# Reciprocal sums multiplied into the exponentials on GpSimd, and post mixing in matmuls of 256 columns

## The chip, the cores and the metric

The kernel runs on one core of a Trainium2 chip. The metric is the device time of one execution in microseconds; three runs were taken and the median is quoted. Beside them stands one execution under the hardware profiler, from which all rows of the trace come. The engines are called TensorE (PE in the profile, its weight loads PEld), VectorE (DVE), ScalarE (ACT), GpSimd (POOL) and SyncE (SP).

## The reference

Talking-heads attention (the heads are mixed before and after the softmax) for 4 batches, 12 heads, 448 positions and 64 channels per head, and then a mixer block: a token MLP over the 448 positions and a channel MLP over the 768 channels, both with a residual.

```python
scores = scale * np.matmul(q, k.transpose(0, 1, 3, 2))
scores = np.einsum('bhij,hg->bgij', scores, w_pre)
scores = scores - np.max(scores, axis=-1, keepdims=True)
attn = np.exp(scores)
attn = attn / (np.sum(attn, axis=-1, keepdims=True) + 1e-09)
attn = np.einsum('bhij,hg->bgij', attn, w_post)
x = np.matmul(attn, v)               # then heads side by side: (4, 448, 768)
h = np.maximum(x.transpose(0, 2, 1) @ w_tok1, 0.0) @ w_tok2
u = x + h.transpose(0, 2, 1)
out = u + np.maximum(u @ w_ch1, 0.0) @ w_ch2
```

## The kernel before

The attention is cut into 16 tiles (4 batches, each with 120, 120, 120 and 88 query rows), and a tile into groups of 10 query rows (the last of a batch ends with a group of 8). A group holds 10 rows of all 12 heads in 120 partitions. `steps` are one or two groups; there are 92 of them, 88 with two groups and 4 with one. The order of all instructions is written by hand (`manual_schedule`): the loop near the end of the attention issues, for step `i`:

- `regroup`: DMAs on SyncE that gather the score rows of later groups into one of 8 buffers `rt`.
- `pre` of step `i + 2`: matmuls with `kpre`, which mix the heads before the softmax, into PSUM (`PP`). `x` counts the two halves of a group's 10 rows, 5 rows and 12 heads (60 partitions of 64) each, `s` the groups of the step.
- `rec` of step `i + 1`: on VectorE 1e-9 is added to the sums (one instruction for each `x`) and the reciprocals are taken; then GpSimd multiplies `kpost` (the weights of the mixing after the softmax, 128 x 64) with the reciprocals, once for each `x`, into the tiles `wr`.
- `mx` of step `i + 2` (row maxima, VectorE), then for some steps `qk` (a later tile's scores, TensorE, copied out of PSUM by ScalarE), then `ex` of step `i + 2` (exponentials with their sums, ScalarE, one for each `x`, into one of the 6 tiles `et`).
- `post` of step `i`: matmuls with `wr` as weights, of 128 columns, 16 for each `x` where the step has two groups. Each stands as two instructions in the trace, each with a weight load of its own.
- `turn` of step `i`: VectorE transposes the result out of PSUM, in 32 x 32 blocks, into `AT`.
- `av` for some steps: the product of a finished tile's weights with `v`, for a pair of heads, from the tile before. Its result leaves PSUM by a copy on ScalarE and, by `settle` in the next step, an add on VectorE.

PSUM tiles of `qk`, `post` and `av` take turns in two buffers (`ps_w`), those of `pre` in two others. From the last tile of the attention on, `cv_tick` converts the weights of the mixer block, a unit at a time, on ScalarE, VectorE and GpSimd (`cv_clamp` and the low half in `cv_step`). The token MLP (`tok1`, `tok2`) and the channel MLP (`ch1`, `ch2`) follow; the change does not touch them.

Of the kernel before, what the change touches and what calls it, by code (L numbers as in the profile page):

```python
# [8 lines left out]
F32 = mybir.dt.float32  # L9
F32R = mybir.dt.float32r  # L10
BF16 = mybir.dt.bfloat16
I32 = mybir.dt.int32
U32 = mybir.dt.uint32
ACTF = mybir.ActivationFunctionType
ALU = mybir.AluOpType
# [4 lines left out]
B, H, S, D = 4, 12, 448, 64  # L20
DM = H * D
DT, DC = 256, 1536
JT = 4
# [1 line left out]
GR = 10  # L25
HP = H // 2
NR = 8
NE = 6
KD = DM // 128
NC = DC // 128  # L30
WARM = 11
# [6 lines left out]
def attn_mixer_kernel(  # L38
# [12 lines left out]
    nc = tc.nc  # L51
# [24 lines left out]
    mid = en("mid", bufs=2)  # L76
# [3 lines left out]
    kcat = [mid.tile([128, 34], F32, bufs=1, name=f"kcat{i}") for i in range(2)]  # L80
    kpre = mid.tile([128, 64], F32, bufs=1, name="kpre")
    kpost = mid.tile([128, 64], F32, bufs=1, name="kpost")
    et = [mid.tile([128, 512], F32, bufs=1, name=f"e{i}") for i in range(NE)]
    rt = [mid.tile([128, S], F32, bufs=1, name=f"r{i}") for i in range(NR)]
    AT, V = {}, {}

    K = {}
    Q = {}
    S_t, R, E, SM, WR, PP, PO = {}, {}, {}, {}, {}, {}, {}
    ne = [0]  # L90

    groups = []
# [86 lines left out]
    def ex(st):  # L179
        m = 64 * len(st)  # L180
        s, p = SM[st[0]], PP.pop(st[0])
        E[st[0]] = []
        for x in range(2):
            e = et[ne[0] % NE]
            ne[0] += 1
            nc.scalar.activation(  # L186
                out=e[:m, :S], in_=p[:m, x, :S], func=ACTF.Exp, bias=s[:m, x:x + 1], scale=1.0,
                accum_out=s[:m, 2 + x:3 + x],
            )
            E[st[0]].append(e)  # L190

    def rec(st):
        m = 64 * len(st)
        s = SM.pop(st[0])
        for x in range(2):
            nc.vector.tensor_scalar_add(out=s[:m, 4 + x:5 + x], in0=s[:m, 2 + x:3 + x], scalar1=1e-9)  # L196
        nc.vector.reciprocal(out=s[:m, 6:8], in_=s[:m, 4:6])  # L197
        WR[st[0]] = []
        for x in range(2):
            r = mid.tile([128, 64], F32, tag="wr", bufs=4, name="wr")  # L200
            nc.gpsimd.tensor_scalar(  # L201
                out=r[:m], in0=kpost[:m], scalar1=s[:m, 6 + x:7 + x], scalar2=None, op0=ALU.mult,
            )
            WR[st[0]].append(r)

    def post(st):
        p = pair("w", "post")
        for x, (e, w) in enumerate(zip(E.pop(st[0]), WR.pop(st[0]))):
            ek = e.rearrange("p (m a r) -> p m a r", m=JT, a=4)
            for hf in range(2):  # L210
                o = 256 * x + 128 * hf
                for a in range(4):
                    for s in range(len(st)):
                        k = slice(64 * s, 64 * s + 64)
                        nc.tensor.matmul(  # L215
                            out=p[32 * a:32 * a + 32, s, o:o + 128], lhsT=w[k, 32 * hf:32 * hf + 32],
                            rhs=ek[k, :, a, :], start=True, stop=True,
                        )
        PO[st[0]] = p

    def turn(st):
# [16 lines left out]
    def av(T, hp):  # L238
        settle()
        b, t = divmod(T, 4)  # L240
        i0, n = IT[t]
        w = 24 if t < 3 else 18
        at_ = AT[T].rearrange("p c (x f) -> p (c x) f", x=2)
        p = pair("w", "av")
        for j in range(JT):
            for r in range(2 if j < 3 else 1):
                k = slice(64 * r, 64 * r + 64)
                for s in range(2):
                    h = 2 * hp + s
                    f = 128 * (h // 6) + 32 * j + 5 * (h % 6)  # L250
                    nc.tensor.matmul(  # L251
                        out=p[64 * s:64 * s + 64, r, :5 * w], lhsT=V[b][k, h, j, :], rhs=at_[k, :w, f:f + 5],
                        start=j == 0, stop=j == 3 - r,
                    )
        x = late.tile([128, 120], F32, tag="x", bufs=6, name="x")
        m = n // GR * GR
        cols = [(x[:, :m].rearrange("p (k c) -> p c k", k=GR), lambda y: y[:, :m].rearrange("p (c k) -> p c k", k=GR))]
        if m < n:
            cols.append((x[:, m:n], lambda y: y[:, m + 1:n + 1]))
        for o, v_ in cols:  # L260
            nc.scalar.copy(out=o, in_=v_(p[:, 0]))

        def add():
            for o, v_ in cols:
                nc.vector.tensor_tensor(out=o, in0=v_(p[:, 1]), in1=o, op=ALU.add)
            nc.sync.dma_start(out=x_dr[b][:, hp, i0:i0 + n], in_=x[:, :n])

        pend.append(add)
# [11 lines left out]
    for r in rt:  # L280
        nc.gpsimd.memset(r[:4], 0.0)
    load_q(1, one)
    wz = et[0].bitcast(BF16)
    for e in et:
        nc.vector.memset(e if e is et[0] else e[:, S:], 0.0)
    for i in range(WARM):
        p = pair("w", "pw")
        nc.tensor.matmul(out=p[:120, 0], lhsT=wz[:120, :120], rhs=wz[:120, 120:632], start=True, stop=True)
# [2 lines left out]
    for x in range(2):  # L291
        ps_ = slice(64 * x, 64 * x + 64)
        nc.vector.tensor_tensor(
            out=kpre[ps_, :60].rearrange("p (i g) -> p i g", i=5),
            in0=kcat[0][ps_, :12].unsqueeze(1).to_broadcast([64, 5, H]),
            in1=mask[0][ps_, 5 * x:5 * x + 5].unsqueeze(2).to_broadcast([64, 5, H]), op=ALU.mult,
# [3 lines left out]
    for s in range(2):  # L300
        ps_ = slice(64 * s, 64 * s + 64)
        for hf in range(2):
            nc.gpsimd.tensor_tensor(
                out=kpost[ps_, 32 * hf:32 * hf + 30].rearrange("p (g i) -> p g i", g=6),
# [138 lines left out]
    for T in range(2, NT):  # L443
        f = sf[T - 2]
# [239 lines left out]
```

## Time and profile before

| | us |
|---|---|
| median of 3 runs | 835.3 |
| lowest, highest | 832.13, 836.86 |
| profiled execution | 840.8 |
| its span, first to last instruction | 839.0 |

Times in the rows are microseconds from the start of the span unless marked ns. In a timeline a row is a run of equal instructions of one engine, with its start, its length and, in brackets, the idle time of the engine before it and what ended it; "issue" means that the profile shows nothing that was waited for. Matmuls are pipelined and their ends are modelled. In a table of stretches each engine has its busy time and the number of its instructions; PEclk is the granted clock of TensorE as a share of the full one. A name such as post<-e,wr gives what an instruction writes and what it reads. The attention steps take the stretch from about 25 to 388 us.

### The profile page before, as it was taken

To read this page: it belongs to the slowest core of one execution; us is meant where nothing else is said; L and a number is where in the kernel's file an instruction comes from. 1 tells how busy PE (TensorE), PEld (TensorE's weight loads), DVE (VectorE), ACT (ScalarE), POOL (GpSimd) and SP (SyncE) were. 2 spreads that over 40 slices of the span, in tenths; PEclk is the share of its full clock that TensorE was granted. 3 is DMA by queue.
4 is the path that set the end of the run, shared out by engine and by line. 5 is a ranking of instruction groups with operands and counts; after the bars stand their busy time and mean duration, and the time that the engine had idled before them with its cause. 6 is when DMAs were issued, how large, how long until landed. Compare 5 with 4: busy or idle time off the path is not lost.

```text
span 839.0 us, 28093 instructions
## 1 busy us (share of the span) xinstructions
PE 799.1 (95%) x12091; PEld 619.8 (74%) x12091; DVE 478.1 (57%) x970; ACT 339.2 (40%) x817; POOL 194.6 (23%) x292
## 2 busy tenths in 40 slices
PE   7898898999999899987999999999999999999998
PEld 3455564666556565655788899999999999999997
DVE  3876576777777577886789999973000400030002
ACT  3666565666656566644455434431000200010000
POOL 3222121222222122223626777730000000000000
PEclk9999999999999999997799999999999999999999
DMA  5674456654765455365456676644000300010001
GB/s 170 204 227 138 117 166 194 212 134 146 224 194 145 113 181 179 128 145 185 134 170 225 184 204 176 172 151 169 1 1 1 132 0 1 1 67 1 1 0 66
DMA packets 63388, 106.05 MB, mean 126 GB/s; under 512 B 21747, under 2 KB 49952, under 8 KB 62752
## 3 DMA queue, kind: packets, MB, share of 16 engines
q1 hardware_dynamic: 62848, 103.35, 40.0%
q8 instruction: 95, 1.56, 0.8%
q10 hardware_dynamic: 320, 0.87, 0.4%
q14 instruction: 29, 0.24, 0.1%
q0 software_dynamic: 96, 0.03, 0.0%
HBM read 49.18 MB, written 16.52 MB: 78 GB/s over the span
## 4 chain that ended last, share of the span: by engine, by line
PE 51%; DVE 1%; ACT 0%; issue 0%
PE pc L522 7%; PE pc L521 7%; PE pc L523 7%; PE po L522 7%; PE po L521 7%; PE po L523 7%; PE pt L521 3%; PE pt L522 2%; PE pt L523 2%; PE pt L536 1%; PE tr L506 1%; PE av L251 1%; DVE ur L622 0%; PE pt L535 0%; DVE h L518 0%; DVE xn L513 0%
## 5 line engine op out<-in xcount | busy, mean ns | idle before, releaser
L518 DVE SCALAR_TENSOR_TENSOR rl<-pc,rh 128x448 fp32r<-128x448 f32 x48 | 29.8, 622 | 221.6 <-ACT rh L517 221.6
L228 DVE STREAM_TRANSPOSE at<-post 128x1024 f32<-128x1024 f32 (+1 forms) x92 | 112.8, 1226 | 73.3 <-PE post L215 73.1
L215 PEld LDWEIGHTS post<-e,wr 64*32 64x32 f32 x5760 | 84.6, 106 | 84.4 <-POOL wr L201 57.0
L201 POOL TENSOR_SCALAR wr<-kpost,sm 128x64 f32<-128x64 f32 (+1 forms) x184 | 79.0, 445 | 290.2 <-DVE sm L197 148.1
L186 ACT ACTIVATE e<-pre,sm 128x448 f32<-128x448 f32 (+1 forms) x184 | 115.2, 634 | 24.8 <-DVE sm L176 24.6
L215 PE MATMUL post<-e,wr 64*32 64x128 f32 x5760 | 114.3, 276 | 10.7 <-issue 7.1
L517 ACT ACTIVATE rh<-pc 128x448 fp32r<-128x448 f32 x48 | 26.1, 543 | 238.4 <-PE pc L523 238.4
L251 PE MATMUL av<-at,v 64*64 64x120 f32 (+1 forms) x2688 | 104.7, 274 | 14.1 <-issue 9.1
L148 ACT COPY s<-qk 120x896 f32<-120x896 f32 (+1 forms) x84 | 75.5, 906 | 95.0 <-PE qk L141 88.1
L169 PE MATMUL pre<-r,kpre 60*64 60x448 f32 (+1 forms) x720 | 108.1, 563 | 3.6 <-DMA r<-s 2.0
L141 PE MATMUL qk<-k,q 64*64 64x448 f32 (+2 forms) x768 | 104.1, 552 | 5.1 <-issue 1.8
L176 DVE TENSOR_REDUCE sm<-pre 128x2 f32<-128x896 f32 (+1 forms) x92 | 100.1, 1088 | 10.5 <-PE pre L169 6.4
L251 PEld LDWEIGHTS av<-at,v 64*64 64x64 f32 x2688 | 81.3, 137 | 32.4 <-issue 13.8
L522 PE MATMUL pc<-u,w 128*128 128x448 f32 x288 | 105.2, 365 | 0.0
L521 PE MATMUL pc<-u,w 128*128 128x448 f32 x288 | 105.2, 365 | 0.0
L523 PE MATMUL pc<-u,w 128*128 128x448 f32 x288 | 105.2, 365 | 0.0
L523 PE MATMUL po<-rh,w 128*128 128x448 f32 x288 | 105.2, 365 | 0.0
L521 PE MATMUL po<-rh,w 128*128 128x448 f32 x288 | 105.2, 365 | 0.0
L522 PE MATMUL po<-rl,w 128*128 128x448 f32 x288 | 105.2, 365 | 0.0
L390 POOL TENSOR_SCALAR cv_g<-cv_g 128x384 f32<-128x384 f32 (+2 forms) x56 | 87.1, 1556 | 21.7 <-ACT cv_g L384 21.7
L141 PEld LDWEIGHTS qk<-k,q 64*64 64x64 f32 (+2 forms) x768 | 37.2, 130 | 44.7 <-DVE sm L196 26.7
L521 PEld LDWEIGHTS pc<-u,w 128*128 128x128 f32 x288 | 54.1, 188 | 4.4
(70 smaller groups left out, 981.2 us busy)
## 6 DMA issues: line engine op xcount, KB each, us to landing
r<-s SPq DMA_DIRECT2D x176, 210.0 KB
cv_r<-in_w_ch_dram SPq DMA_DIRECT2D x48, 384.0 KB
v<-in_v_dram SPq DMA_DIRECT2D x16, 384.0 KB
xr<-x_dr SPq DMA_DIRECT2D x8, 672.0 KB
u_dr<-u SPq DMA_DIRECT2D x24, 224.0 KB
ur<-u_dr SPq DMA_DIRECT2D x4, 1344.0 KB
out_dram<-ur SPq DMA_DIRECT2D x24, 224.0 KB
k<-in_k_dram SPq DMA_DIRECT2D x21, 224.0 KB
```

Of the source, the lines that this page charges most:

```text
L141: nc.tensor.matmul(out=p[c:c + m, s, :S], lhsT=Q[T][r, h, c:c + m], rhs=K[b][r, h, :], start=True, stop=True)
L169: nc.tensor.matmul(out=p[64 * s:64 * s + 64, x, :S], lhsT=kpre[k], rhs=rt[a % NR][k], start=True, stop=True)
L176: nc.vector.tensor_reduce(out=s[:m, 0:2], in_=PP[st[0]][:m, :, :S], axis=AX.X, op=ALU.max, negate=True)
L186: nc.scalar.activation(out=e[:m, :S], in_=p[:m, x, :S], func=ACTF.Exp, bias=s[:m, x:x + 1], scale=1.0, accum_out=s[:m, 2 + x:3 + x],)
L201: nc.gpsimd.tensor_scalar(out=r[:m], in0=kpost[:m], scalar1=s[:m, 6 + x:7 + x], scalar2=None, op0=ALU.mult,)
L215: nc.tensor.matmul(out=p[32 * a:32 * a + 32, s, o:o + 128], lhsT=w[k, 32 * hf:32 * hf + 32], rhs=ek[k, :, a, :], start=True, stop=True,)
L228: nc.vector.transpose(out=AT[T][:, c:c + w].rearrange("p c f -> p (c f)"), in_=p[:, :w].rearrange("p c f -> p (c f)"))
L251: nc.tensor.matmul(out=p[64 * s:64 * s + 64, r, :5 * w], lhsT=V[b][k, h, j, :], rhs=at_[k, :w, f:f + 5], start=j == 0, stop=j == 3 - r,)
L390: nc.gpsimd.tensor_scalar(out=g[:P], in0=g[:P], scalar1=MAG_MIN, scalar2=MAG_MAX, op0=ALU.max, op1=ALU.min,)
L521: nc.tensor.matmul(out=p, lhsT=a[0], rhs=x[0], start=first, stop=False)
L522: nc.tensor.matmul(out=p, lhsT=a[0], rhs=x[1], start=False, stop=False)
L523: nc.tensor.matmul(out=p, lhsT=a[1], rhs=x[0], start=False, stop=last)
```

## The change

The reciprocals are no longer multiplied into the weights `kpost` but into the exponentials themselves, in place, by one GpSimd instruction for a step (2 x 448 columns, both `x` at once). With that the weights of `post` are `kpost` for both `x`, and one matmul takes the 128 columns of both: 256 columns, 16 matmuls for a step of two groups in place of 32. The two exponentials of a step now lie in one tile, so there are 3 tiles `et` of double width in place of 6. The two sums get their 1e-9 in one VectorE instruction. The order of the result's columns in `AT` changes with it, and `av` reads its operand with three strides (12 x 2 x 5) in place of two (24 x 5).

```diff
-NE = 6
+NE = 3
...
-    et = [mid.tile([128, 512], F32, bufs=1, name=f"e{i}") for i in range(NE)]
+    et = [mid.tile([128, 2, 512], F32, bufs=1, name=f"e{i}") for i in range(NE)]
...
     def ex(st):
         m = 64 * len(st)
         s, p = SM[st[0]], PP.pop(st[0])
-        E[st[0]] = []
+        e = et[ne[0] % NE]
+        ne[0] += 1
         for x in range(2):
-            e = et[ne[0] % NE]
-            ne[0] += 1
             nc.scalar.activation(
-                out=e[:m, :S], in_=p[:m, x, :S], func=ACTF.Exp, bias=s[:m, x:x + 1], scale=1.0,
+                out=e[:m, x, :S], in_=p[:m, x, :S], func=ACTF.Exp, bias=s[:m, x:x + 1], scale=1.0,
                 accum_out=s[:m, 2 + x:3 + x],
             )
-            E[st[0]].append(e)
+        E[st[0]] = e
 
     def rec(st):
         m = 64 * len(st)
-        s = SM.pop(st[0])
-        for x in range(2):
-            nc.vector.tensor_scalar_add(out=s[:m, 4 + x:5 + x], in0=s[:m, 2 + x:3 + x], scalar1=1e-9)
+        s, e = SM.pop(st[0]), E[st[0]]
+        nc.vector.tensor_scalar_add(out=s[:m, 4:6], in0=s[:m, 2:4], scalar1=1e-9)
         nc.vector.reciprocal(out=s[:m, 6:8], in_=s[:m, 4:6])
-        WR[st[0]] = []
-        for x in range(2):
-            r = mid.tile([128, 64], F32, tag="wr", bufs=4, name="wr")
-            nc.gpsimd.tensor_scalar(
-                out=r[:m], in0=kpost[:m], scalar1=s[:m, 6 + x:7 + x], scalar2=None, op0=ALU.mult,
-            )
-            WR[st[0]].append(r)
+        nc.gpsimd.tensor_tensor(
+            out=e[:m, :, :S], in0=e[:m, :, :S], in1=s[:m, 6:8].unsqueeze(2).to_broadcast([m, 2, S]), op=ALU.mult,
+        )
 
     def post(st):
         p = pair("w", "post")
-        for x, (e, w) in enumerate(zip(E.pop(st[0]), WR.pop(st[0]))):
-            ek = e.rearrange("p (m a r) -> p m a r", m=JT, a=4)
-            for hf in range(2):
-                o = 256 * x + 128 * hf
-                for a in range(4):
-                    for s in range(len(st)):
-                        k = slice(64 * s, 64 * s + 64)
-                        nc.tensor.matmul(
-                            out=p[32 * a:32 * a + 32, s, o:o + 128], lhsT=w[k, 32 * hf:32 * hf + 32],
-                            rhs=ek[k, :, a, :], start=True, stop=True,
-                        )
+        ek = E.pop(st[0]).rearrange("p x (m a r) -> p x m a r", m=JT, a=4)
+        for hf in range(2):
+            for a in range(4):
+                for s in range(len(st)):
+                    k = slice(64 * s, 64 * s + 64)
+                    nc.tensor.matmul(
+                        out=p[32 * a:32 * a + 32, s, 256 * hf:256 * hf + 256], lhsT=kpost[k, 32 * hf:32 * hf + 32],
+                        rhs=ek[k, :, :, a, :], start=True, stop=True,
+                    )
...
-        w = 24 if t < 3 else 18
-        at_ = AT[T].rearrange("p c (x f) -> p (c x) f", x=2)
+        w = 12 if t < 3 else 9
+        at_ = AT[T].rearrange("p c (g x f) -> p g c x f", g=2, x=2)
...
-                    f = 128 * (h // 6) + 32 * j + 5 * (h % 6)
+                    f = 32 * j + 5 * (h % 6)
                     nc.tensor.matmul(
-                        out=p[64 * s:64 * s + 64, r, :5 * w], lhsT=V[b][k, h, j, :], rhs=at_[k, :w, f:f + 5],
+                        out=p[64 * s:64 * s + 64, r, :10 * w], lhsT=V[b][k, h, j, :],
+                        rhs=at_[k, h // 6, :w, :, f:f + 5],
```

On TensorE a step in the middle of the attention stands like this before, from its post to the next step's pre (what stands in brackets are the engines and DMA queues whose semaphores are waited for):

```order
L215 MATMUL post<-e_89,wr 32x128 [waits DVE_49,Pool_49]
L215 MATMUL post<-e_89,wr 32x128 x15
L215 MATMUL post<-e_90,wr 32x128 [waits Pool_49]
L215 MATMUL post<-e_90,wr 32x128 x15
L251 MATMUL av<-at,v 64x120 [waits Activation_49]
L251 MATMUL av<-at,v 64x120 x13
```

The changed kernel has there, its lines 207 (post), 243 (av) and 169 (pre):

```order
L207 MATMUL post<-e_91,kpost 32x256 [waits DVE_49,Pool_49]
L207 MATMUL post<-e_91,kpost 32x256 x15
L243 MATMUL av<-at,v 64x120 [waits DMAHW3_49,Activation_49]
L243 MATMUL av<-at,v 64x120 x13
L169 MATMUL pre<-r_97,kpre 64x448 [waits DMAHW4_49]
L169 MATMUL pre<-r_98,kpre 64x448 [waits DMAHW5_49]
```

Post has 16 rows of matmuls in place of 32 and waits for GpSimd once; the order around it is the same.

On GpSimd the last steps of the attention, where the conversion of the mixer's weights begins (cv_g is its clamp), read before:

```order
L201 TENSOR_SCALAR wr_7127<-kpost_88,sm_7017 128x64
L201 TENSOR_SCALAR wr_7129<-kpost_88,sm_7017 128x64
L201 TENSOR_SCALAR wr_7198<-kpost_88,sm_7133 128x64
L201 TENSOR_SCALAR wr_7200<-kpost_88,sm_7133 128x64
L390 TENSOR_SCALAR cv_g_7190<-cv_g_7190 128x256
L201 TENSOR_SCALAR wr_7271<-kpost_88,sm_7204 64x64
L201 TENSOR_SCALAR wr_7273<-kpost_88,sm_7204 64x64
```

and now:

```order
L196 TENSOR_TENSOR e2_91<-e2_91,sm_5287 128x2x448
L196 TENSOR_TENSOR e0_89<-e0_89,sm_5383 128x2x448
L383 TENSOR_SCALAR cv_g_5424<-cv_g_5424 128x256
L196 TENSOR_TENSOR e1_90<-e1_90,sm_5434 64x2x448
L383 TENSOR_SCALAR cv_g_5476<-cv_g_5476 128x256
```

One wide product stands where two narrow ones stood; the clamps stay between the same steps.

## Rows read from the trace of the kernel before

**Rows 1.** The page, busy time of each engine.

```profile
PE 799.1 (95%) x12091; PEld 619.8 (74%) x12091; DVE 478.1 (57%) x970; ACT 339.2 (40%) x817; POOL 194.6 (23%) x292
```

**Rows 2.** Timeline of one full step (start, length, engine, line, operation).

```profile
340.67 1.16 PE L215 MATMUL post<-e,wr 64*32 64x128 f32 x64
...
341.78 0.98 PE L251 MATMUL av<-at,v 64*64 64x120 f32 x26
341.96 1.25 DVE L228 STREAM_TRANSPOSE at<-post 128x1024 f32<-128x1024 f32 x1 [0.69 <-PE post L215]
...
342.50 0.59 PE L169 MATMUL pre<-r,kpre 60*64 60x448 f32 x2
...
343.30 1.07 PE L141 MATMUL qk<-k,q 64*64 64x448 f32 x8
343.34 0.17 DVE L197 RECIPROCAL sm<-sm 128x2 f32<-128x2 f32 x1
...
343.70 0.86 POOL L201 TENSOR_SCALAR wr<-kpost,sm 128x64 f32<-128x64 f32 x2 [2.78 <-PE pre L169]
...
344.30 0.45 PE L215 MATMUL post<-e,wr 64*32 64x128 f32 x16
```

**Rows 3.** Waits of TensorE, 24.8 to 392 us: total, times, longest.

```profile
PE av L251 <- issue: 9.1, 6, 2.8
PE post L215 <- issue: 7.1, 14, 1.3
...
PE qk L141 <- issue: 1.8, 1, 1.8
PE pre L169 <- issue: 1.0, 1, 1.0
```

**Rows 4.** Stretches: length, busy time (instructions) of each engine, PEclk, DMA share, GB/s.

```profile
24.80:388.00 363.20, 339.04 (x9655) 210.65 (x9656) 262.76 (x571) 220.20 (x560) 81.55 (x192) 0.98 0.57 171
100.20:103.70 3.50, 3.50 (x28) 1.79 (x32) 2.01 (x6) 0.40 (x2) 0.86 (x2) 0.51 0.30 104
...
380.10:390.40 10.30, 9.76 (x162) 7.96 (x162) 5.16 (x11) 2.88 (x9) 2.27 (x4) 0.50 0.65 243
```

**Rows 5.** DMA queues, 24.8 to 388 us: packets, MB, share of 16 engines.

```profile
q1 hardware_dynamic: 44686, 60.80, 55.6%
q8 instruction: 75, 1.23, 1.4%
```

**Rows 6.** Timeline of TensorE, two of the gaps.

```profile
99.24 1.06 PE L251 MATMUL av<-at,v 64*64 64x120 f32 x28 [1.91 <-issue]
...
284.02 2.00 PE L251 MATMUL av<-at,v 64*64 64x120 f32 x37 [2.08 <-issue]
```

**Rows 7.** Timeline of steps without qk, the second with a gap.

```profile
357.26 1.16 PE L215 MATMUL post<-e,wr 64*32 64x128 f32 x64
357.39 0.17 DVE L197 RECIPROCAL sm<-sm 128x2 f32<-128x2 f32 x1
...
360.13 0.41 PE L215 MATMUL post<-e,wr 64*32 64x128 f32 x5
360.49 0.17 DVE L197 RECIPROCAL sm<-sm 128x2 f32<-128x2 f32 x1
...
361.82 1.11 PE L215 MATMUL post<-e,wr 64*32 64x128 f32 x59 [1.28 <-issue]
...
364.63 0.73 PE L215 MATMUL post<-e,wr 64*32 64x128 f32 x33
```

**Rows 8.** Timeline, post of a step of one group.

```profile
205.05 1.08 PE L215 MATMUL post<-e,wr 64*32 64x128 f32 x32
```

**Rows 9.** Groups of GpSimd by shape: count, busy, mean ns, idle before and releaser.

```profile
L390 POOL TENSOR_SCALAR cv_g<-cv_g 128x384 f32<-128x384 f32 x48 | 78.4, 1634 | 20.1 <-ACT cv_g L384 20.1
...
L416 POOL TENSOR_TENSOR w<-cv_a,w 128x384 fp32r<-128x384 f32 x16 | 16.5, 1028 | 33.4 <-ACT w L399 32.8 <-PE pt L536 0.6
...
L416 POOL TENSOR_TENSOR t<-cv_a,t 128x256 fp32r<-128x256 f32 x4 | 2.9, 729 | 10.7 <-ACT t L399 10.7
```

More of the change, by code (lines that the diff above doesn't have):

```diff
@@ L88, in attn_mixer_kernel @@
     Q = {}
-    S_t, R, E, SM, WR, PP, PO = {}, {}, {}, {}, {}, {}, {}
+    S_t, R, E, SM, PP, PO = {}, {}, {}, {}, {}, {}
     ne = [0]
@@ L282, in attn_mixer_kernel @@
     load_q(1, one)
-    wz = et[0].bitcast(BF16)
+    wz = et[0][:, 0].bitcast(BF16)
     for e in et:
-        nc.vector.memset(e if e is et[0] else e[:, S:], 0.0)
+        nc.vector.memset(e if e is et[0] else e[:, :, S:], 0.0)
     for i in range(WARM):
```

## Prediction

> **What bounds the kernel now.** I read the page first: TensorE is busy 95% of the span [rows 1]. Busy is not the same as unhindered, so next came the timeline of one undisturbed step. There the order on TensorE is post at 340.67 us, av at 341.78, pre at 342.50, qk at 343.30 and the next post at 344.30 [rows 2]: 1.11 + 0.72 + 0.80 + 1.00 = 3.63 us, with no hole. A second loop has the same length: post, then VectorE's transpose (341.96, 1.25 us, ending at 343.21), for which qk waits at 343.30, then qk, then post. GpSimd works 0.86 us of the step. So a step is bound by TensorE and by post, transpose and qk at once, and neither the small products on GpSimd nor VectorE's sums end last.
>
> Not all steps are like this one. The list of waits has TensorE idle on "issue", that is for nothing that the profile shows, 9.1 us before av, 7.1 before post, 1.8 before qk and 1.0 before pre: **19.0 us in 22 gaps** [rows 3]. What is missing there must be the instructions themselves. In the stretch of the attention steps TensorE ran 9655 matmuls and 9656 weight loads [rows 4], and the instruction queue q8 moved 75 packets of together 1.23 MB in the same stretch [rows 5]: 19,311 / 75 = 257 instructions a packet. The queue is TensorE's, and it brings 256 instructions at a time.
>
> The Trainium skill has a rule that speaks against this reading, and so against any gain from fewer instructions: "Runtime: NRT & Kernel Launch", section "Instruction fetch mechanics", says that blocks of 256 instructions are fetched while the block before is executed, and that the fetch is hidden because dispatch is slower than the refill. The trace agrees on the 256 and shows 22 gaps where it isn't hidden; by the rule the gaps had another cause and would stay, which is the first rival below.
>
> **Gaps.** A full step without disturbance issues, with the weight loads, 128 instructions for post, 56 for av, 16 for pre and 16 for qk: 216 in 3.63 us, so a packet lasts 256 / 216 x 3.63 = 4.3 us. The change halves those of post: 64 + 56 + 16 + 16 = 152, so a packet lasts 6.1 us. If a fetch takes as long as before, each gap shrinks by 1.8 us. Only those above that leave anything: 1.83 (the one before qk, 1.8 in the list), 1.91 and 2.08 [rows 6], and the longest, 2.75 (2.8 in the list) [rows 3]. That is 0.03 + 0.11 + 0.28 + 0.95 = 1.4 us of 19.0. Steps without qk give 200 instructions in 2.87 us before and 136 after, 3.7 and 5.4 us a packet, which is much the same. Bounds: nothing saved (rival 1) and all 19.0.
>
> Each gap costs more than it shows, because the view counts idle time only from the modelled end of the matmul before. In steps without qk the undisturbed distance of two posts is 360.13 - 357.26 = 2.87 us; the next, with a gap of 1.28 us inside, is 364.63 - 360.13 = 4.50 [rows 7]: 1.63 lost, 0.35 more than shown. For 22 gaps that is up to 7.7 us; since some of it hides in waits for the transpose I take 6.
>
> **Clock.** Behind the gap of 1.91 us the granted clock was 0.51, the lower of its two levels (1.2 of 2.4 GHz), for 3.5 us, and behind the longest gap 0.50 for 10.3 us [rows 4]; the gap of 2.08 us is followed by the like of the first. Behind the gap of 1.28 us post still took 1.11 us [rows 7]. TensorE was busy almost throughout these windows, so half of the two short ones is lost, 3.5 us together, and of the long one, part of which is copies at their own pace, some 4 us: 7.5 in all. With the gaps at most 1 us long this should go too; the bound below is that all of it stays.
>
> Lost to gaps: 19.0 + 6 + 7.5 = 32.5 us. What remains (1.4, and as much again for hidden time and slack that I count too high) is 3, so **29.5 us come back**.
>
> **Post in 256 columns.** Streamed columns stay the same, half as many matmuls of twice the length. Before, the 64 matmuls of a post take 1.16 us [rows 2]. A post of one group alone has 32 matmuls, as long, on half the array's rows. If the number of instructions set the time, it would take about half; it takes 1.08 us [rows 8]. So columns set it and little is saved: between 0 and 0.05 us a step, 92 steps; I take 0.02, **-2 us**. Av's operand is cut in three strides where there were two, over the same 5-element runs; nothing in the trace prices that, and I take 0 (from 0 to 0.05 us on av's 0.72, 96 times, 5 us).
>
> **Product on GpSimd.** New in each step is one product of 2 x 448 elements in place of two of 64. The nearest rows are the same operation at 384 and 256 columns, 1028 and 729 ns: 2.34 ns an element and 0.13 us fixed, so 0.13 + 896 x 2.34 = **2.23 us**. The upper bound is the slowest row of GpSimd, 1634 ns for 384 columns: 896 x 4.26 = 3.8 us [rows 9]. The lower is 64 columns at 445 ns, which says no more than that it is not free.
>
> Behind it waits post of the next step. In the full step the reciprocal starts at 343.34, GpSimd at 343.70, so the product ends at 345.93; the post that reads it is the one after 344.30, at 347.93 [rows 2]. Cover 2.0 us, cost 0. In steps without qk the reciprocal starts at 357.39; GpSimd follows 0.36 us later, so the product ends at 359.98, and its post stands at 360.13 [rows 7]: cover 0.15 us. There VectorE and ScalarE turn at 360.49 - 357.39 = 3.10 us a step, against 2.87 on TensorE, and have so far lived on their lead. With the lead used up those steps take 3.10: 8 in the last tile, 0.23 each, 2 us. The first post has no step ahead of it to hide in and pays the difference, 2.23 - 0.86 = 1.4 us; at the end the last product is queued on GpSimd behind the one before and a clamp, another 1.5 by my estimate. Sum **+5 us**, from 0 to 10.
>
> VectorE loses one small sum per step. It idles 0.69 us before the transpose [rows 2], so that is worth 0. Buffers of the exponentials are as deep as before (three pairs for six singles).
>
> **Sum.** The profiled execution took 840.8 us: 840.8 - 29.5 - 2 + 5 = 814.3. The runs before have a median of 835.3, 5.5 lower. If that is fewer gaps, there is that much less to win, and the new kernel's runs lie close to its profile; I take 1.3 below: **813 us**.
>
> **Rivals.**
> 1. The gaps are not the fetch, or dispatch is the limit in another way. Then only -2 + 5 is left: 835.3 + 3 = 838. For it: some gaps fall inside av, not post. Against: 257 instructions a packet. 12%.
> 2. Slower: the product paces the steps. It decides from 3.6 us on, when GpSimd needs more than the 3.63 of a step. At the upper bound of 3.8 us, plus 0.05 between two, it costs 0.2 us in some 70 steps and 0.98 in some 20: 34 us, and of the gaps 27 come back: 835.3 + 34 - 27 + 2 = 844. For it: a two-operand instruction with a repeated scalar is not in the trace. Against: the same operation at 2.34 ns. 7%.
> 3. Half. The fetch waits behind the bulk transfers (q1 took 55.6% of 16 engines in the stretch [rows 5]); steps closer together fill it more, fetches take longer, and half of the 29.5 stays. 835.3 - 15 + 3 = 823, up to 830 with the halved clock. 13%.
>
> **How the numbers follow.** The forecast has 67%, and 1% is for none of these. A measurement of this kernel tells about 0.5% from no change, so 831.1 and 839.5 are the limits. Faster: 67 + 13 = 80%. Same: rival 1, 12%. Slower: rival 2 and the remainder, 8%. The range takes the forecast and rival 3: low when no gap remains, post saves its full 5 and GpSimd costs nothing (835.3 - 29.5 - 5 = 801, nearly all at once, so 803); high at rival 3's end, 830.
>
> **What would show it.** Right: q8 with some 22 packets fewer; idle on "issue" of TensorE at 1 to 4 us; no half clock at 100 and 284 us; post still 1.1 us; the product near 2.2 us, ending before its post in the full step; steps of 3.6 us as before. Wrong: gaps of the old size with half the post instructions, the list of waits naming GpSimd's product before post in full steps, or a product above 3.6 us.

## The result, and the profile after

| | before | after |
|---|---|---|
| median of 4 runs each, us | 834.0 | 810.6 |
| lowest, highest | 832.13, 836.86 | 809.46, 813.02 |
| profiled execution, us | 840.8 | 809.6 |
| its span | 839.0 | 807.8 |

The kernel before has one run more here than ahead of the prediction. The ratio is 0.972, with an interval of 0.968 to 0.976: 2.8% faster. The forecast was 813.0 us, with a range of 803 to 830.

Three lines of the page of the changed kernel: busy time, share and number of instructions of each engine; the clock granted to TensorE in 40 slices, in tenths; the queue that brings TensorE's instructions (packets, MB, share).

```profile
PE 780.5 (97%) x9211; PEld 576.4 (71%) x9211; DVE 474.8 (59%) x875; ACT 337.3 (42%) x817; POOL 270.0 (33%) x200
...
PEclk9999999999999999997999999999999999999999
...
q8 instruction: 72, 1.18, 0.6%
```

Against [rows 1] TensorE has 2880 matmuls and as many weight loads fewer. GpSimd is busy 75 us more, and TensorE is nearer to full than before.

All of the difference lies in the attention steps. The next lines give a stretch of each kernel, from its first post to the end of its last: length, then busy time and count of PE, PEld, DVE, ACT and POOL, granted clock, DMA share, GB/s. First before, then after.

```profile
24.80:386.60 361.80, 337.64 (x9629) 209.27 (x9631) 261.43 (x568) 220.20 (x560) 81.55 (x192) 0.98 0.57 171
```

```profile
25.90:356.90 331.00, 321.26 (x6748) 168.22 (x6748) 257.59 (x475) 217.15 (x557) 155.98 (x99) 0.99 0.61 180
```

361.8 - 331.0 = 30.8 us, of 31.2 between the two spans. TensorE's busy time fell by 16.4 us and its idle time by 14.4 (24.2 to 9.7), less than the 19.0 on issue [rows 3], since other waits grew.

The waits of TensorE in the changed kernel, 24.8 to 392 us (total, times, longest), answer [rows 3]:

```profile
PE av L243 <- DVE x L258: 3.6, 4, 1.2
PE av L243 <- DVE at L220: 2.3, 4, 0.9
PE post L207 <- ACT s L148: 2.2, 6, 0.4
PE post L207 <- DVE at L220: 1.8, 4, 0.8
PE post L207 <- POOL e L196: 1.7, 1, 1.7
PE pre L169 <- DMA r<-s: 1.2, 1, 1.2
```

No row on "issue" is left: 19.0 us in 22 gaps became none. Post waits for GpSimd's product once, at the first post. The wait for a gather is new; it stands at 43.16 us and is followed by a granted clock of 0.51 from 44.5 to 47.9 us, so that this one step took 6.44 us.

A full step after the change, to be read against [rows 2] (start, length, engine, line; idle time before and what ended it in brackets):

```profile
306.01 1.09 PE L207 MATMUL post<-e,kpost 64*32 64x256 f32 x32
306.17 0.91 ACT L148 COPY s<-qk 120x896 f32<-120x896 f32 x1 [1.17 <-PE qk L141]
...
307.12 0.86 PEld L243 LDWEIGHTS av<-at,v 64*64 64x64 f32 x28 [0.50 <-ACT s L148]
...
307.21 1.25 DVE L220 STREAM_TRANSPOSE at<-post 128x1024 f32<-128x1024 f32 x1 [0.61 <-PE post L207]
...
307.86 0.59 PE L169 MATMUL pre<-r,kpre 60*64 60x448 f32 x2
...
308.66 1.08 PE L141 MATMUL qk<-k,q 64*64 64x448 f32 x8
...
308.88 1.68 POOL L196 TENSOR_TENSOR e<-e,sm 128x896 f32<-128x896 f32 x1 [1.94 <-DVE sm L195]
...
309.67 1.09 PE L207 MATMUL post<-e,kpost 64*32 64x256 f32 x32
```

Post is 0.06 us shorter, yet the step is 3.66 us; the median of the 52 full steps after 100 us is 3.61, and was 3.62. The product takes 1.68 us and ends at 310.56; the post that reads it is the one after 309.67, at 313.27.

### The profile page after: what moved, and what is told of

Its sections match the earlier page's. It is cut to its first block, busy times and chain, and to the rows that moved or that the text cites. A ratio compares the mean times of both kernels' runs of the same rounds, so it can differ in the third digit from the quotient of the medians.

```text
span 807.8 us, 22146 instructions
## 1 busy us (share of the span) xinstructions
PE 780.5 (97%) x9211; PEld 576.4 (71%) x9211; DVE 474.8 (59%) x875; ACT 337.3 (42%) x817; POOL 270.0 (33%) x200
## 4 chain that ended last, share of the span: by engine, by line
PE 88%; DVE 6%; ACT 2%; DMA 2%; issue 1%; POOL 0%; SPq 0%; DVEq 0%; ACTq 0%
PE post L207 10%; PE av L243 9%; PE pre L169 8%; PE qk L141 8%; PE pc L514 7%; PE pc L516 7%; PE pc L515 7%; PE po L516 7%; PE po L514 7%; PE po L515 7%; PE pt L514 3%; PE pt L515 2%; PE pt L516 2%; DVE sm L176 2%; DVE at L220 2%
## 5 line engine op out<-in xcount | busy, mean ns | idle before, releaser
L196 POOL TENSOR_TENSOR e<-e,sm 128x896 f32<-128x896 f32 (+1 forms) x92 | 154.6, 1680 | 189.9 <-DVE sm L195 157.3
L243 PEld LDWEIGHTS av<-at,v 64*64 64x64 f32 x2688 | 78.1, 134 | 50.4 <-ACT s L148 35.9
L169 PE MATMUL pre<-r,kpre 60*64 60x448 f32 (+1 forms) x720 | 105.2, 556 | 3.3 <-DMA r<-s 3.2
L243 PE MATMUL av<-at,v 64*64 64x120 f32 (+1 forms) x2688 | 100.1, 269 | 8.4 <-DVE x L258 3.6
L207 PE MATMUL post<-e,kpost 64*32 64x256 f32 x2880 | 100.9, 383 | 6.2 <-ACT s L148 2.2
L207 PEld LDWEIGHTS post<-e,kpost 64*32 64x32 f32 x2880 | 45.9, 106 | 82.8 <-issue 54.1
L141 PE MATMUL qk<-k,q 64*64 64x448 f32 (+2 forms) x768 | 100.8, 548 | 1.8 <-DVE s L146 0.9
```

The costliest lines, as they stand in the source:

```text
L141: nc.tensor.matmul(out=p[c:c + m, s, :S], lhsT=Q[T][r, h, c:c + m], rhs=K[b][r, h, :], start=True, stop=True)
L169: nc.tensor.matmul(out=p[64 * s:64 * s + 64, x, :S], lhsT=kpre[k], rhs=rt[a % NR][k], start=True, stop=True)
L196: nc.gpsimd.tensor_tensor(out=e[:m, :, :S], in0=e[:m, :, :S], in1=s[:m, 6:8].unsqueeze(2).to_broadcast([m, 2, S]), op=ALU.mult,)
L207: nc.tensor.matmul(out=p[32 * a:32 * a + 32, s, 256 * hf:256 * hf + 256], lhsT=kpost[k, 32 * hf:32 * hf + 32], rhs=ek[k, :, :, a, :], star ...
L243: nc.tensor.matmul(out=p[64 * s:64 * s + 64, r, :10 * w], lhsT=V[b][k, h, j, :], rhs=at_[k, h // 6, :w, :, f:f + 5], start=j == 0, stop=j ...
```

## Experiments

Each was compared with the kernel before on the same chip (medians of before 836.4, 838.5, 838.3 and 837.0 us in the four sets). "Stretch" is the length from the first post to the end of the last, worked out from the timeline; it and the idle time come from one profiled execution each.

| run | median us | ratio, interval | stretch us | idle on issue us |
|---|---|---|---|---|
| before | 834.0 | | 361.7 | 19.0 |
| after | 810.6 | 0.972 (0.968 to 0.976) | 330.9 | 0 |
| e1_product_128 | 837.7 | 1.003 (1.000 to 1.007) | 358.0 | 18.8 |
| e2_no_product | 810.9 | 0.973 (0.968 to 0.979) | 331.8 | 0 |
| e3_light_gather | 825.1 | 0.991 (0.987 to 0.994) | 346.4 | 9.5 |
| e4_light_gather_after | 806.0 | 0.968 (0.965 to 0.972) | 326.9 | 0 |
| e5_half_256 | 825.6 | 0.989 (0.982 to 0.996) | 347.5 | 1.5 |
| e8_half_256_x_outer | 817.5 | 0.977 (0.973 to 0.982) | 330.6 | 0 |
| e6_product_twice | 836.2 | 1.000 (0.996 to 1.003) | 355.2 | 0 |
| e9_product_twice_no_add | 816.6 | 0.978 (0.972 to 0.984) | 335.9 | 0 |
| e7_product_on_vector | 874.7 | 1.048 (1.040 to 1.056) | 394.0 | 0 |
| e10_score_copy_shared | 827.3 | 0.988 (0.985 to 0.991) | 348.5 | 0 |
| e11_av_behind_pre | 823.2 | 0.985 (0.980 to 0.990) | 343.7 | 0 |
| e12_after_again | 808.6 | 0.967 (0.962 to 0.972) | 331.4 | 0 |

### One part alone: the product, with post in 128 columns

```diff
-        for hf in range(2):
-            for a in range(4):
-                for s in range(len(st)):
...
-                        out=p[32 * a:32 * a + 32, s, 256 * hf:256 * hf + 256], lhsT=kpost[k, 32 * hf:32 * hf + 32],
-                        rhs=ek[k, :, :, a, :], start=True, stop=True,
...
+        for x in range(2):
+            for hf in range(2):
+                o = 256 * hf + 128 * x
+                for a in range(4):
+                    for s in range(len(st)):
...
+                            out=p[32 * a:32 * a + 32, s, o:o + 128], lhsT=kpost[k, 32 * hf:32 * hf + 32],
+                            rhs=ek[k, x, :, a, :], start=True, stop=True,
```

> The changed kernel with its product on GpSimd kept, but post again in matmuls of 128 columns: TensorE's instructions are those of before, everything else is as after the change. If the 19 us of gaps on TensorE were waits for instructions (a packet of 256 lasting 4.3 us a full step instead of 6.1), they come back here: idle on issue 12 to 25 us, some half clock behind the longest, 830 to 842 us. If the gain came from the product's place, the single wait of post or the layout of the exponentials, the time stays at 808 to 815 us with no gaps.

Measured: 837.7 us, no different from before. The waits of its TensorE on issue:

```profile
PE av L245 <- issue: 9.2, 6, 2.6
PE post L209 <- issue: 7.7, 12, 1.9
...
PE pre L169 <- issue: 1.3, 2, 0.9
...
PE qk L141 <- issue: 0.6, 1, 0.6
```

That is 18.8 us in 21 gaps where before had 19.0 in 22, with the old number of instructions. Everything else of the change is in this kernel, so the gain comes from the halved number of post's matmuls.

That a gap is a wait for an instruction packet can also be read from the two traces themselves. Number TensorE's matmuls and weight loads from 0 in the order of their starts: all 22 gaps of the kernel before stand at the same place of a block of 256, number 193 or 194, and each ends 1.29 to 1.63 us after a packet of q8 has landed. The 21 gaps here stand at the same two places, 1.17 to 1.68 us after a packet.

### The product left out

```diff
-        nc.gpsimd.tensor_tensor(
-            out=e[:m, :, :S], in0=e[:m, :, :S], in1=s[:m, 6:8].unsqueeze(2).to_broadcast([m, 2, S]), op=ALU.mult,
-        )
```

The division by the sums is missing in this kernel; post reads the exponentials as they are.

> The changed kernel without the product on GpSimd, so the division by the sums is left out. If the product is covered in full steps (it ends some 2.7 us before its post) and costs only at the first post, in the steps without qk and in the last steps, 804 to 809 us. If it slows VectorE or ends late in full steps too, more than 10 us come off: below 800 us.

Measured: 810.9 us, against 810.6 with the product: a gain of 2 to 6 us was expected and none is seen. The interval of the ratio, 0.968 to 0.979, is some 5 us to either side, so the times alone don't settle it. The traces do: from the seventh step to the end of the last post the two take the same time (309.8 us without the product, 309.6 with it). The timeline shows why: two slow steps without qk are as slow without the product, each held back by VectorE's transpose.

```profile
341.25 1.10 PE L204 MATMUL post<-e,kpost 64*32 64x256 f32 x32 [0.24 <-DVE at L217]
344.36 1.10 PE L204 MATMUL post<-e,kpost 64*32 64x256 f32 x32 [0.25 <-DVE at L217]
```

344.36 - 341.25 = 3.11 us; the same steps of the changed kernel:

```profile
339.50 1.10 PE L207 MATMUL post<-e,kpost 64*32 64x256 f32 x32 [0.24 <-DVE at L220]
...
342.62 1.10 PE L207 MATMUL post<-e,kpost 64*32 64x256 f32 x32 [0.24 <-DVE at L220]
```

3.12 us. The product is hidden there too. Of the steps without qk one is longer with it, 2.97 us (from 333.4 us) against 2.80.

### Fewer bytes beside the instructions

If a gap is a fetch that comes too late, the gathers, which move most bytes of these steps, may be what delays it. Two kernels gather three of a group's twelve heads after the first eight groups (the other rows keep old data), before and after.

```diff
-        nc.sync.dma_start(out=rt[G % NR][o:o + 12 * n], in_=rows(G)(S_t[4 * b + t], 0))
+        w = H if G < NR else 3
+        nc.sync.dma_start(out=rt[G % NR][o:o + w * n], in_=rows(G)(S_t[4 * b + t], 0)[:, :w])
```

> The kernel before with the gather of score rows cut to a quarter of its bytes after the first 8 groups (three of twelve heads; the other rows keep old scores). TensorE's instructions are unchanged. If the gaps are instruction packets that queue behind the bulk transfers, fetches get shorter and over half of the gaps go: idle on issue under 8 us, 811 to 824 us. If the gaps come from the number of instructions alone (dispatch), they stay: some 19 us of idle, 830 to 838 us.

> The same cut of the gather in the changed kernel, as the control of the run before. With no gaps left there is nothing to win from shorter fetches: 806 to 811 us. If the gather itself was on the path (pre waiting for its rows), it falls by as much as the kernel before does with the cut.

Measured: 825.1 us for the kernel before with the cut. Its waits on issue, and the share of q1 (against [rows 3] and [rows 5]):

```profile
PE av L252 <- issue: 4.8, 4, 2.7
...
PE pre L170 <- issue: 2.7, 2, 1.7
...
PE post L216 <- issue: 2.0, 4, 0.9
```

```profile
q1 hardware_dynamic: 29155, 33.20, 33.3%
```

9.5 us in 10 gaps remain, half of the 19.0, with as many instructions. The cut by itself is worth 4.0 us in the stretch (330.9 to 326.9, after); before it was worth 15.3 (361.7 to 346.4). So some 11 us come from the gaps: they depend on what else the DMA engines carry as well as on the number of instructions. I had expected less than 8 us to be left, so light traffic alone does not cure it.

### Half of the narrow matmuls back

```diff
-                    nc.tensor.matmul(
-                        out=p[32 * a:32 * a + 32, s, 256 * hf:256 * hf + 256], lhsT=kpost[k, 32 * hf:32 * hf + 32],
-                        rhs=ek[k, :, :, a, :], start=True, stop=True,
-                    )
+                    for x in ((slice(0, 2),), (slice(0, 1), slice(1, 2)))[hf]:
+                        o = 256 * hf + 128 * x.start
+                        nc.tensor.matmul(
+                            out=p[32 * a:32 * a + 32, s, o:o + 128 * (x.stop - x.start)],
+                            lhsT=kpost[k, 32 * hf:32 * hf + 32], rhs=ek[k, x, :, a, :], start=True, stop=True,
+                        )
```

> The changed kernel with the first half of post (hf 0) in matmuls of 256 columns and the second in two of 128: 24 matmuls a step, 184 instructions a full step, 5.05 us a packet. If each gap shrinks by the time by which a packet lasts longer, 0.75 us against before, about 7 us of idle on issue are left and the time lies between the two kernels, 815 to 828 us. If the length of post's matmuls or its one wait is what counts, either all or none of the gain is there: under 813 or over 832 us.

The time, 825.6 us, looked like half of the effect, but the trace says otherwise: only 1.5 us of gaps were left, and post had become longer. With x innermost, two narrow matmuls in a row use the same 64 x 32 part of the array.

```profile
301.60 1.35 PE L209 MATMUL post<-e,kpost 64*32 64x256 f32 x48
```

A time that fits an expectation for another reason settles nothing, so the half was made again with x outside:

```diff
-        for hf in range(2):
+        for hf, xs in ((0, (0, 2)), (1, (0, 1)), (1, (1, 2))):
+            o, w = 256 * hf + 128 * xs[0], 128 * (xs[1] - xs[0])
...
-                        out=p[32 * a:32 * a + 32, s, 256 * hf:256 * hf + 256], lhsT=kpost[k, 32 * hf:32 * hf + 32],
-                        rhs=ek[k, :, :, a, :], start=True, stop=True,
+                        out=p[32 * a:32 * a + 32, s, o:o + w], lhsT=kpost[k, 32 * hf:32 * hf + 32],
+                        rhs=ek[k, xs[0]:xs[1], :, a, :], start=True, stop=True,
```

> The changed kernel with half of post back in narrow matmuls: the first 32 rows of each result in 256 columns, the second in two matmuls of 128 with x outermost, so that two matmuls in a row never fall on the same part of the array (in the half-way version before, they did, and post took 1.35 us). A full step then has 96 + 56 + 16 + 16 = 184 instructions, a packet of 256 lasts 256 / 184 x 3.63 = 5.05 us, 0.75 us longer than before the change. Theory (a gap is a fetch that takes longer than the packet lasts): each gap is some 0.75 us shorter than with 216 instructions; of the 22 gaps with 19 us some 3 to 8 us are left on issue, post is at 1.08 to 1.16 us, time 814 to 826. Rival (the narrow matmuls cost time by themselves, in proportion): half of the difference between 810.6 and 837.7, so 824, with post between 1.09 and 1.16 and as many gaps as before at half the length or less. Rival (only 256 columns throughout help): 835.

Its post, and the stretch of its steps:

```profile
304.80 1.15 PE L208 MATMUL post<-e,kpost 64*32 64x256 f32 x48
```

```profile
28.70:359.40 330.70, 322.37 (x8188) 191.66 (x8188) 257.34 (x475) 217.22 (x557) 155.84 (x99) 1.00 0.61 180
```

Post is as long as before the change (1.15 against 1.16), the steps take what they take after it (330.7 against 331.0 us), and there is no gap. Two things follow. The shorter post is worth nothing in a full step (the median is 3.61 us in both kernels) and 0.05 us in a step without qk (2.85 against 2.80). And at 184 instructions a full step the gaps are nearly gone, none here and 1.5 us in the half-way kernel before, where 3 to 8 us had been expected to stay. The whole time is 6.9 us above the changed kernel's all the same. In the profiled executions, 8.7 us apart, 2.8 us stand ahead of the first post (28.7 against 25.9), and nearly all of the rest in the channel MLP, which no edit touched: one group of its matmuls, here and in the changed kernel (count, busy us, mean ns, idle before):

```profile
L515 PE MATMUL pc<-u,w 128*128 128x448 f32 x288 | 106.0, 368 | 0.0
```

```profile
L514 PE MATMUL pc<-u,w 128*128 128x448 f32 x288 | 105.2, 365 | 0.0
```

The six such groups take turns. From the first to the last of their 1728 matmuls it is 357.3 us here and 350.4 in the changed kernel, 6.8 us more; their starts are 206.7 ns apart in place of 202.7, at the full granted clock in both. Why they differ stays open.

### The product twice

The price of a slow product was the prediction's slower rival. A second product, by ones, doubles GpSimd's work.

```diff
+    ones = mid.tile([128, 2], F32, bufs=1, name="ones")
+    nc.gpsimd.memset(ones, 1.0)
...
+        nc.gpsimd.tensor_tensor(
+            out=e[:m, :, :S], in0=e[:m, :, :S], in1=ones[:m].unsqueeze(2).to_broadcast([m, 2, S]), op=ALU.mult,
+        )
```

> The changed kernel with a second product on GpSimd in each step, the exponentials times one (1.68 us more). Full steps have some 2.7 us of cover and stay at 3.62 us; steps without qk (2.7 to 3.1 us) become paced by GpSimd at some 3.5 us, about 20 of them with 0.4 to 0.8 us each: 818 to 828 us. If the product is covered everywhere, under 814 us; if it already sets the full steps, above 850 us.

Measured: 836.2 us, full steps of 3.83 us where 3.62 had been expected, since 3.4 us of products are still less than a step. The timeline around the second product and VectorE's addition of 1e-9 (L196 here):

```profile
300.53 1.68 POOL L201 TENSOR_TENSOR e<-e,ones 128x896 f32<-128x896 f32 x1
...
301.39 0.84 DVE L196 TENSOR_SCALAR sm<-sm 128x2 f32<-128x2 f32 x1
...
302.27 0.17 DVE L197 RECIPROCAL sm<-sm 128x2 f32<-128x2 f32 x1
...
302.61 1.68 POOL L198 TENSOR_TENSOR e<-e,sm 128x896 f32<-128x896 f32 x1 [0.40 <-PE qk L143]
```

An addition of two columns lasts 0.84 us and ends at 302.23, when the product ends (302.21). Over the stretch its mean is 728 ns, against 135 in the changed kernel, where none begins during a product. So the addition and the products take turns: two products and the space between them, 3.43 us, and 0.40 from the end of the one to the next, 3.83. The Trainium skill, "SBUF — State Buffer", section "Who interferes with whom", says that GpSimd shares a pair of ports with VectorE, that whoever is first holds it for its whole instruction, and that tensor_scalar is among the operations that may want it. The 0.84 us agree with that.

To test it, the addition was left out (the reciprocal reads the sums, so 1e-9 is missing), with both products:

```diff
-        nc.vector.tensor_scalar_add(out=s[:m, 4:6], in0=s[:m, 2:4], scalar1=1e-9)
-        nc.vector.reciprocal(out=s[:m, 6:8], in_=s[:m, 4:6])
+        nc.vector.reciprocal(out=s[:m, 6:8], in_=s[:m, 2:4])
```

> Two products a step on GpSimd (the second by ones), as in the run that took 836.2 us, and VectorE's addition of 1e-9 to the sums left out: the reciprocal reads the sums directly. Theory (the small addition on VectorE is the one instruction that is held until GpSimd's product has ended, which ties VectorE's and GpSimd's steps together at 2 x 1.68 + the rest = 3.83 us): without it full steps are back at 3.60 to 3.66 us, and the time is 812 to 824 (more than the changed kernel, since steps without qk are still paced by 3.4 us of products, some 10 times 0.3 to 0.6 us). Rival (two products of 3.4 us with the way from reciprocal to post are too long by themselves): full steps stay at 3.8 us, 833 to 838. Third: the reciprocal is held in the place of the addition; its time in the profile then rises from 0.17 to about 0.8 us and the total stays near 836.

Measured: 816.6 us, 20 us less for an instruction of 0.13 us. Full steps are back at 3.60 to 3.64 us. The reciprocal is not held in its place: 73 of these begin during a product and last 128 ns in the mean, the others 129.

```profile
L196 DVE RECIPROCAL sm<-sm 128x2 f32<-128x2 f32 x87 | 11.2, 129 | 3.6 <-ACT e L187 3.6
```

Steps without qk are now paced by the products, as this post of one shows (335.01 to 338.41 us, 3.40 a step):

```profile
335.01 1.10 PE L211 MATMUL post<-e,kpost 64*32 64x256 f32 x32 [0.40 <-POOL e L200]
```

### The product on VectorE

```diff
-        nc.gpsimd.tensor_tensor(
+        nc.vector.tensor_tensor(
```

> The changed kernel with the product on VectorE in place of GpSimd. VectorE is idle some 0.6 us before the transpose of a full step, and a product of 896 columns should take 1.1 to 1.5 us there, by its 638 ns for 384: the transpose starts 0.5 to 0.9 us later and qk behind it, 845 to 880 us. If VectorE had room for it, under 820 us.

Measured: 874.7 us, within what was expected. The operation takes 1092 ns there, less than GpSimd's 1680, but it stands ahead of av's add and the maxima, and post waits 64 times for that add, for the place in PSUM:

```profile
PE post L207 <- DVE x L258: 42.2, 64, 1.1
```

GpSimd is the slower engine for it and the right one.

### Two attempts on what binds a step now

In a full step av waits for ScalarE's copy of the scores, and qk for the transpose. First, VectorE took a quarter of that copy:

```diff
-            nc.scalar.copy(out=S_t[T][:n, h::HP, :], in_=p[:n, :, :S])
+            nc.scalar.copy(out=S_t[T][:n, h::HP, :336], in_=p[:n, :, :336])
+            nc.vector.tensor_copy(out=S_t[T][:n, h::HP, 336:], in_=p[:n, :, 336:S])
```

> The changed kernel, with VectorE copying the last 112 of 448 columns of a qk result and ScalarE only the first 336 (ScalarE alone took 0.91 us). It tells apart what sets a full step now that post takes 1.09 us for 1.16 and steps are still 3.62. Theory A (av waits for ScalarE's copy of the scores, which ends last there: post to av 1.11 us in steps with qk, 1.02 without): the copies end 0.15 to 0.2 us earlier, post to av falls to 1.02 to 1.06, steps to 3.53 to 3.58, and the time to 803 to 807. Theory B (the other loop sets it: post, VectorE's transpose, qk that waits for the transpose to free its place in PSUM, post: 1.09 + 0.11 + 1.25 + 0.20 + 1.01 = 3.66): av starts earlier and qk waits that much longer; steps stay at 3.60 to 3.66 and the time at 809 to 812. Slower, 815 to 830, if VectorE's extra copy delays the transpose.

Measured: 827.3 us. The two copies did not run side by side:

```profile
328.71 1.09 PE L208 MATMUL post<-e,kpost 64*32 64x256 f32 x32
328.87 0.72 ACT L148 COPY s<-qk 88x672 f32<-88x672 f32 x1 [1.17 <-PE qk L141]
329.62 0.39 DVE L149 COPY s<-qk 88x224 f32<-88x224 f32 x1 [0.32 <-ACT s L148]
...
330.07 0.97 PE L244 MATMUL av<-at,v 64*64 64x120 f32 x26 [0.26 <-DVE s L149]
```

VectorE's begins when ScalarE's has ended, and together they last longer than the one (0.72 + 0.03 + 0.39 against 0.91). The edit did not do what it says and leaves both theories untested. It shows one thing: av starts 1.36 us after post in place of 1.11, and the step is 3.86 us in place of 3.62. A delay of av, 0.25 us, is a delay of the step, 0.24 us, with no slack.

Second, av was put behind the next step's pre, where it need not wait for that copy:

```diff
+        if i and i <= sf[NT - 1]:
+            for a in value[i - 1]:
+                av(*a)
         if i + 1 < len(steps):
             rec(steps[i + 1])
...
         turn(st)
-        for a in value[i]:
-            av(*a)
+        if i >= sf[NT - 1]:
+            for a in value[i]:
+                av(*a)
```

> The changed kernel with av moved one place later on TensorE: a step's av stands behind the next step's pre, and its add on VectorE before that step's mx (in the last tile as before). Post is then followed by pre, which needs no copy of ScalarE, where it was followed by av, which waits for the place that qk's scores leave in PSUM. TensorE's work alone is 0.80 (pre) + 0.74 (av) + 1.01 (qk) + 1.02 (post) = 3.57 us against 3.62 measured in a full step. Theory A (what binds a step now is that wait of av for ScalarE's copy, 1.11 us from post to av where 1.02 would do): full steps of 3.55 to 3.58 us, some 70 steps by 0.05 us, 805 to 809. Theory B (the loop of post, transpose, qk and post binds as well, and now the add of av is a new link in it): steps stay at 3.60 us or grow, 810 to 825.

> The changed kernel as it is, on the same chip as the run with av behind pre, to set that run against: 809 to 813, full steps of 3.60 to 3.64 us, no idle time on issue.

Measured: 823.2 us, against 808.6 for the changed kernel in the same set. Post now waits for what follows av:

```profile
315.90 0.37 ACT L254 COPY x<-av 128x120 f32<-128x120 f32 x1 [0.62 <-PE av L243]
316.30 0.37 DVE L258 TENSOR_TENSOR x<-av,x 128x120 f32<-128x120 f32 x1 [0.62 <-ACT x L254]
...
316.81 1.10 PE L207 MATMUL post<-e,kpost 64*32 64x256 f32 x32 [0.22 <-DVE x L258]
```

Av ends at 315.84, its copy at 316.27, its add at 316.67, and post, which needs av's place in PSUM, starts at 316.81: 3.82 us a step. One wait was given up for a longer one. Neither attempt beat the changed kernel.

## Why the prediction was right

**What bounds the kernel, and the gaps: right.** The reading that the 22 gaps are late instructions, from 257 instructions a packet, is what the run in 128 columns bears out: the same work in twice as many matmuls brings the 19 us back. The places of the gaps, one in 256 instructions and each just behind a packet, say the same. Rival 1, that the gaps have another cause, falls with it. So does, as far as this kernel goes, the rule of the Trainium skill ("Runtime: NRT & Kernel Launch", section "Instruction fetch mechanics") that the fetch is hidden. q8 has 52 packets in the shorter stretch, 24.8 to 356 us, where it had 75 [rows 5]: 23 fewer, and 22 had been named.

**The size of what stays: too cautious, and by a model that is too simple.** By "each gap shrinks by 1.8 us" 1.4 us should have stayed; nothing did. The sum had a fetch last as long as before. The transfers do: 0.88 to 1.69 us before, with a median of 1.07, and 0.99 in the median after. What varies is when one starts. Before, a packet starts in the median 1.35 us after the first instruction of the block ahead of its own, but ahead of the four longest gaps 3.8 to 4.7 us after it, and there the transfer itself takes only 0.88 to 0.97 us. So the long gaps are late starts that the block being executed does not outlast. The changed kernel's blocks last 6.09 us in the median, as the prediction has it, and cover even the latest start, at 4.06 us. Counting the packets that land less than 1.7 us ahead of their first instruction, and so leave a gap or nearly one, gives 37 of 73 before, 6 of 64 in each half-way kernel and 1 of 53 after. In the first half-way kernel a start 4.85 us late still left a gap of 1.3 us; all nine profiled executions at 152 instructions have none in the attention steps.

What makes a start late is not shown, only what it goes with: in the 3 us ahead of a start that is over 2.2 us late q1 took 0.69 of the 16 DMA engines, ahead of one under 1.2 us late 0.45. With the lighter gathers 14 packets of 75 started over 2 us late where 23 of 73 had, and half of the gaps went. This is the force that rival 3 named (half of the gaps stay, since fetches wait behind bulk transfers), and q1 did rise, from 55.6% to 59.3%; at 152 instructions a step it no longer matters.

**Clock: right in what it names.** No stretch at the lower level is left at 100 and 284 us, and the one of 10.3 us behind the longest gap [rows 4] is gone too. One stays behind the attention, 0.51 from 368.5 to 379 us; before it stood there too, 0.51 from 397 to 411. New is the one at 44.5 us, behind the wait for a gather; that step cost 2.8 us more than a full one.

**Post in 256 columns: the time right, the worth wrong.** It is 1.09 us for 1.16, a little more than the 0.05 us allowed as the most. But the sum took 2 us off the path for it, and the half-way run, with post at 1.15 and the same stretch, shows about 0: nothing in full steps, 0.05 us in each of ten or so without qk. In full steps av starts 1.11 us after post, when ScalarE's copy of the scores has ended, and it was so before:

```profile
340.83 0.90 ACT L148 COPY s<-qk 88x896 f32<-88x896 f32 x1 [1.16 <-PE qk L141]
...
341.78 0.85 PEld L251 LDWEIGHTS av<-at,v 64*64 64x64 f32 x28 [0.22 <-ACT s L148]
```

The copy ends at 341.73 us, av's weights follow at 341.78, and post had started at 340.67. The prediction had looked for what waits on the product and on qk, and not for what else av waits for when post gets shorter.

**The product: right place, too dear.** Sized 2.23 us, measured:

```profile
L196 POOL TENSOR_TENSOR e<-e,sm 128x896 f32<-128x896 f32 x88 | 147.9, 1680 | 183.9 <-DVE sm L195 151.6 <-PE pre L169 31.2 <-ACT s L145 1.1
```

The 2.34 ns an element came from products with a converted result [rows 9]; this one, in float32 and in place, takes 1.68 us for 896 elements. The cost of +5 us became about 0: in the run without it the stretch from the seventh step on is no shorter. The first post waits 1.68 us where it waited 0.76, so 0.9 of the 1.4 named. Two of the steps without qk take 3.11 us, which the prediction had from VectorE's and ScalarE's loop, but so they do with no product at all: that loop was rightly read, and wrongly put down to the product.

**The slower rival: its deciding point was wrong.** It was said to decide from 3.6 us on. With the addition of 1e-9 on VectorE held until the product ends, 0.40 us come on top of GpSimd's own time in each step, and the point is, by this estimate, near 3.63 - 0.40 = 3.2 us. Two products of together 3.4 us passed it and gave back the whole gain. At 1.68 us it was never near, so the forecast did not suffer; without the addition the 3.4 us leave full steps alone, as the prediction's reckoning has it.

**The sum.** Forecast from the profiled execution: 840.8 - 29.5 - 2 + 5 = 814.3; measured 809.6. The stretch gave 30.8 us back, where the terms add up to 26.5. The run in 128 columns, which has the product but not the wide matmuls, puts 27.1 us on their number (358.0 to 330.9, one execution each), so the 29.5 for gaps, hidden time and clock were about right together; how they divide was not measured. The terms -2 and +5 were both near 0, and that their errors partly cancel is luck.

## What to carry to other kernels

When TensorE idles on "issue" with nothing that it waits for, divide its instructions by the packets of its instruction queue, and count whether the gaps stand whole packets apart: if they do, packets are used up faster than they come, and fewer and wider matmuls pay even where the columns, and the matmuls' own time, stay the same. Work moved to GpSimd is priced by the VectorE instructions that may be held while it runs, a tiny one among them, and not by its duration alone. When a time agrees with an expectation, look in the trace whether it came the expected way, as the half-way run did not.

## What the runs showed of the hardware

- Gaps on issue stand whole blocks of 256 TensorE instructions apart and end 1.17 to 1.68 us after a q8 packet has landed. They are 19 us at 216 instructions in a full step, 0 and 1.5 us at 184, none at 152. With q1's share down from 55.6% to 33.3% they halve at the old rate.
- The transfer of a packet takes 0.88 to 1.69 us before; ahead of the longest gaps it isn't slow (0.88 to 0.97) but starts late, 3.8 to 4.7 us into the block ahead of it, where the median is 1.35.
- A post of 48 matmuls takes 1.35 us in an order where narrow matmuls in a row use the same 64 x 32 part of the array, and 1.15 in one where they do not.
- A VectorE tensor_scalar of 128 x 2 that begins while GpSimd multiplies 128 x 896 lasts up to the product's end (mean 728 ns for 135). Maxima and transposes that begin during a product keep their times (1083 and 1249 ns), and so does the reciprocal in the run without the addition (128 ns, 129 beside no product).
- The untouched channel MLP took 368 ns a matmul in place of 365 in the two half-way kernels, 6.8 us from its first to its last; no run here tells why.
